# Block products for the last chunk's second layer, and transposes of the third chunk on TensorE

## The chip, the cores and the metric

One core of a Trainium2 chip. The metric is the time of one execution in device microseconds; the median of three runs of the kernel before is 212.14 us (211.63 to 212.49).

## What is computed

Attention with four sink keys and a window of 128, for 4 batches, 8 heads, 768 positions and head size 64, then a layer norm and a two-layer MLP with a residual:

```
scores = scale * q @ k^T;  keep where key < 4 or 0 <= row - key < 128
a = softmax(scores);  x = (a @ v), heads side by side      # 4 x 768 x 512
xn = (x - mean) / sqrt(var + 1e-6) * g_ln
out = x + relu(xn @ w_ch1) @ w_ch2                         # 512 -> 2048 -> 512
```

## The kernel before

The 3072 tokens are cut into 24 tiles of 128 and 12 chunks of two tiles; three chunks are one batch. For each chunk the kernel loads q and k (`nat`, L722, casting loads that POOL issues), transposes them so that the head size lies on the partitions (`kT`, `qT`), scores, exponentiates (ACT), masks and multiplies with v on TensorE, and normalises on VectorE: `x` (L1046), mean and variance (L900, L902), 1/sigma by a power on POOL (L910, L911), and `xc` (L907 without 1/sigma, L914 with it). `xc` is transposed into `xnt`. The MLP of the chunk has a first layer (`ph`, L1062: 64 matmuls of 128x256, `w1` against `xnt`), a relu into four `h1` tiles (L1073 on ACT, L1075 on VectorE), and a second layer.

From chunk 3 on, attention runs in blocks (`block`, L939): block t multiplies the probabilities of tile t-1 with v (L976 to L992) and then scores tile t (L1003, and L1011 for the sinks, in even tiles). Block 8 thus finishes tile 7, the last one that chunk 3's first layer needs, and scores the first tile of chunk 4.

The transposes of `xc` come in two kinds (`normalise`, L897). Chunks below `x_by_dma` (2 here) use four TensorE transposes a tile (L922); the eviction multiplies by `g_ln` (L933 on VectorE, L934 on ACT). The other chunks use a DMA transpose issued by SP (L925, issued through L595). These have no eviction, so `g_ln` must be in `w1`: after the last chunk with TensorE transposes, 16 operations scale `w1` in place (L1217 on VectorE, L1218 on ACT).

The second layer comes in two kinds. `second` (L1154) multiplies `h1` with `w2`, 16 matmuls for each tile or cut (L1167), then one fused operation adds the residual and multiplies by 1/sigma (L1175), and a store follows (L1179). The last tile is cut at column 320; the first cut is stored by ACT, the last by SP. `second_by_seven` (L1082) takes chunks 3 to 10. It regards the chunk's two tiles, the two halves of the 2048 hidden units and the two halves of the 512 output columns as 2x2 blocks, and makes the four output blocks from seven block products of eight 128x256 matmuls each (L1113) instead of eight. The sums that this needs are made once for `w2` (`w2t`, L1209), and in each chunk for `h1` (L1090, eight on VectorE). PSUM banks b0, b1, b2 hold the products; intermediate results are copied by ACT or VectorE (L1119) or added to an earlier copy (L1123), and `x` is added at the end (L1150). For these chunks `xc` has 1/sigma in it.

What sets the order: every operation is given to a planner (`Plan.run`, L114) with its possible engines, a cost and a priority (a due time). The planner lists the operations of each engine in the order of its own schedule, and the chip executes them so, with semaphores. TensorE, SP and the others each work through one list; a DMA transpose waits on SP behind whatever stands ahead of it. PSUM tiles (`one`, four banks; `pair`, two double banks) and SBUF tiles come from rings.

Of the kernel before, what the change touches and what calls it, by code (L numbers as in the profile page):

```python
# [10 lines left out]
ALU = mybir.AluOpType  # L11
# [194 lines left out]
def dve(n, per=1.04):  # L206
    t = 0.067 + 0.001 * per * n
    return (t, t + 0.09)


def fix(occ, extra=0.09):
# [8 lines left out]
HW_S = (0.75, 0.8, 1.2)  # L220
HW_X = (0.75, 0.2, 1.2)
# [9 lines left out]
NEVER = -1e9  # L231
BIG = 3.3e38

PAR = dict(gk=(5, 4), gv=(4, 5), strict=400.0, win=0.4, tr=-8.0, sc=-5.0, sc1=-2.0, av=2.0, blk=-8.0, step=10.0, trx=9.0, by_dma=4, x_by_dma=2,
           w1p=(1.6, 2.6, 2.7, 2.8), pm=3, w2p=(4.5, 4.51, 4.52, 4.53), apart=2, vs0=(2.0, 13.0), by_tile=0, vp=(0.0, 0.1, 2.0, 2.1, 4.55, 4.56), ld1=0.05, t0=0.8, warm=7.9, pm0=-40.0, w1g=17.0, gtt=1.25, seven=3, lead=(0, 0, 0, 2, 4, 9), w2t=-4.0, at7=(0.5, 1.5, 2.5, 3.5, 4.5, 6.5, 7.5))


# [134 lines left out]
def kernel(  # L372
# [12 lines left out]
    nc = tc.nc  # L385
# [4 lines left out]
    RB = S // 128  # L390
# [6 lines left out]
    NC = B * RC  # L397
# [7 lines left out]
    P = Plan()  # L405
# [110 lines left out]
    def negs(e):  # L516
# [18 lines left out]
         writes=[gr_b], dma=HW_T)  # L535
# [136 lines left out]
    def chunk(c):  # L672
# [37 lines left out]
        else:  # L710
            both = []
            for nm, src, bT in (("k", k, kT_b), ("q", q, qT_b)):
                T = Buf(f"{nm}T{c}", nm + "T")
                bT[c] = T
                if c < PAR["by_dma"]:
                    both.append((nm, src, T, ld + (0.1 if nm == "q" else 0.0)))
                    continue
                for i in range(2):
                    nat = Buf(f"{nm}n{c}{i}", "nat")
                    ap = src[b, :, 256 * R + 128 * i:256 * R + 128 * (i + 1), :].rearrange("h p d -> p h d")  # L720
                    P.op(f"{nm}ld{c}{i}", {"POOL": (0.87, 0.9)}, ld + 0.01 * i + (0.1 if nm == "q" else 0.0),
                         lambda e, nat=nat, ap=ap: G.dma_start(nat.t, ap), writes=[nat], dma=SW_N, after=gate(c))  # L722
                    P.op(f"tr{nm}{c}{i}", {"SP": (1.2, 1.2)}, d + 0.01 * i, lambda e, T=T, nat=nat, i=i: dma_t(
                        T.t[:, :, 128 * i:128 * i + 128], nat.t.rearrange("p h d -> p (h d)")),
                        reads=[nat], writes=[T], dma=HW_X, after=[trx_op[2 * c - 3]] if c > PAR["by_dma"] and nm == "q" else [])
            if both:
                by_pairs(c, both, d)
        if R == 0:
# [353 lines left out]
    def second_by_seven(c, T, h1):  # L1082
# [63 lines left out]
        for i, t in enumerate((t0, t1)):  # L1146
            b, r, x = t // RB, t % RB, x_b[t]
            done = Buf(f"of{t}")
            tail["sum", t] = P.op(f"o{t}", {"POOL": (1.1, 1.2), "DVE": dve(512, 1.06)}, T + 9 + i, lambda e, i=i, x=x: (
                V if e == "DVE" else G).tensor_tensor(ot[i].t, ot[i].t, x.t, op=ALU.add), reads=[ot[i], *oo[i], x], writes=[done])  # L1150
            P.op(f"st{t}", {"SP": (0.54, 0.59)}, T + 9.1 + i, lambda e, i=i, b=b, r=r: nc.sync.dma_start(
                out[b, 128 * r:128 * (r + 1), :], ot[i].t), reads=[ot[i], done], dma=HW_S)

    def second(c, T, h1):  # L1154
        for i in range(2):
# [90 lines left out]
    t = PAR["t0"]  # L1246
# [67 lines left out]
```

## Time and profile before

| | |
|---|---|
| runs | 212.49, 211.63, 212.14 us, median 212.14 |
| profiled execution | 211.49 us, of which the span is 210.0 |
| TensorE busy | 201.6 us |
| VectorE, ACT, POOL busy | 151.7, 121.4, 115.9 us |
| granted TensorE clock | 1.0 |

The span is the time from the first to the last instruction or transfer that the profile shows; the rest of the execution lies around it. Rows of a timeline give the start in us from the beginning of the span, the duration, the engine, the line, the operation, and in square brackets the idle time before it with what ended it. SPq, ACTq and POOLq are the issue of transfers, "DMA" in the chain of waits is a transfer from its issue to its landing. Rows of a group of instructions give the total busy time, the mean of one in ns, and the idle time before them.

### The profile page before, as it was taken

How to read it: one execution, taken by the hardware profiler on the slowest of the kernel's cores; microseconds unless marked ns; L12 is line 12 of the kernel's file. 1: busy time of each engine (PE TensorE's matmuls, PEld its weight loads, DVE VectorE, ACT ScalarE, POOL GpSimd, SP SyncE). 2: the span in 40 equal slices, each digit the busy share in tenths (PEclk: the TensorE clock that was granted, in tenths of full speed). 3: DMA queues.
4: the chain of work that ended last, by engine and by line, in shares of the span. 5: the costliest groups of instructions: out<-in, count | busy, mean ns of one | idle time of the engine just before them, and what ended most of it. 6: DMA issues, size and time to landing. Idle time of an engine off the chain costs nothing.

```text
span 210.0 us, 7046 instructions
## 1 busy us (share of the span) xinstructions
PE 201.6 (96%) x2891; PEld 161.7 (77%) x2891; DVE 151.7 (72%) x413; ACT 121.4 (58%) x212; POOL 115.9 (55%) x170
## 2 busy tenths in 40 slices
PE   7799999999989899899999999999999999999994
PEld 2458975755865688688888888888888888888853
DVE  5599867998845669888789688778778778773121
ACT  3798688283762475386475565665664764453610
POOL 7969942479979757846856792793732102410000
PEclk9999999999999999999999999999999999999999
DMA  5999999999999999999999999999994221120203
GB/s 146 195 186 199 190 208 200 169 187 142 163 193 125 153 153 130 124 204 149 76 185 152 77 158 184 85 152 171 94 174 101 78 78 25 59 71 3 100 0 108
DMA packets 105643, 28.05 MB, mean 134 GB/s; under 512 B 94852, under 2 KB 102664, under 8 KB 105608
## 3 DMA queue, kind: packets, MB, share of 16 engines
q0 software_dynamic: 70960, 13.18, 96.6%
q1 hardware_dynamic: 33448, 13.71, 37.6%
q10 hardware_dynamic: 1200, 0.69, 1.2%
q8 instruction: 23, 0.38, 0.8%
q14 instruction: 12, 0.10, 0.2%
HBM read 27.43 MB, written 6.29 MB: 161 GB/s over the span
## 4 chain that ended last, share of the span: by engine, by line
PE 81%; DMA 11%; DVE 4%; ACT 1%; issue 1%; POOL 1%; ACTq 0%; DVEq 0%; POOLq 0%
PE one L1062 37%; PE one L1113 22%; PE one L1167 11%; DMA xnt<-xc 5%; DMA qT<-nat 4%; DMA natf<-in_q_dram 3%; PE pair L1003 2%; PE one L976 2%; PE one L983 1%; PE one L992 1%; DVE st L900 1%; PE pair L1011 1%; DVE x L892 1%; PE pair L623 1%; PE pair L749 1%
## 5 line engine op out<-in xcount | busy, mean ns | idle before, releaser
L1062 PE MATMUL one<-xnt,w 128*128 128x256 bf16 x768 | 88.4, 273 | 1.6 <-DMA xnt<-xc 1.6
L1062 PEld LDWEIGHTS <-w 128*128 128x128 bf16 x768 | 74.2, 98 | 11.6 <-issue 2.3
L1073 ACT ACTIVATE h<-one 128x512 bf16<-128x512 f32 x92 | 54.8, 599 | 37.2 <-PE one L1062 36.0
L664 POOL DMA_DIRECT2D vn<-in_v_dram x59 | 39.2, 689 | 8.5 <-DMA w<-in_moe_w_ch_dram 6.9
L910 POOL TENSOR_SCALAR st<-st 128x1 f32<-128x1 f32 x24 | 9.8, 410 | 49.4 <-DVE st L902 48.9
L1021 ACT ACTIVATE pe<-pair 128x768 bf16<-128x768 f32 x36 | 27.3, 808 | 15.4 <-PE pair L1003 15.1
L1167 PE MATMUL one<-w,h 128*128 128x512 bf16 (+2 forms) x144 | 29.5, 356 | 0.0
L1167 PEld LDWEIGHTS <-h 128*128 128x128 bf16 x144 | 13.4, 98 | 12.0
L1113 PEld LDWEIGHTS <-h 128*128 128x128 bf16 x192 | 18.4, 98 | 2.7 <-issue 0.3
L1119 ACT COPY tx<-one 128x256 f32<-128x256 f32 x24 | 8.9, 372 | 18.4 <-PE one L1113 18.4
L911 POOL TENSOR_TENSOR st<-st,mhalf 128x1 f32<-128x1 f32 x24 | 16.3, 678 | 2.0
L900 DVE BATCH_NORM_STATS2 st<-x 128x6 f32<-128x512 bf16 x24 | 16.7, 694 | 0.8
L1113 PE MATMUL one<-w,h 128*128 128x256 bf16 x128 | 16.6, 273 | 0.1
L1113 PEld LDWEIGHTS <-sb 128*128 128x128 bf16 x156 | 14.8, 98 | 2.0
L1046 DVE TENSOR_TENSOR x<-one,rec 128x256 bf16<-128x256 f32 x36 | 15.3, 424 | 1.2
L722 POOL DMA_DIRECT2D nat<-in_k_dram x16 | 15.1, 950 | 1.3 <-DMA natp<-in_q_dram 1.3
L1150 DVE TENSOR_TENSOR ot<-ot,x 128x512 f32<-128x512 f32 x15 | 10.4, 692 | 7.2 <-ACT ot L1119 7.0
L722 POOL DMA_DIRECT2D nat<-in_q_dram x16 | 14.4, 912 | 0.0
L1175 DVE SCALAR_TENSOR_TENSOR ot<-one,st,x 128x512 f32<-128x512 f32 (+2 forms) x9 | 6.2, 691 | 11.2 <-PE one L1167 9.9
L1026 DVE TENSOR_TENSOR pe<-pe,band 128x768 bf16<-128x768 bf16 x24 | 12.0, 540 | 0.0
L914 DVE TENSOR_SCALAR xc<-x,st 128x512 bf16<-128x512 bf16 x16 | 6.6, 412 | 7.3 <-POOL st L911 7.3
L1123 DVE TENSOR_TENSOR ot<-one,tx 128x256 f32<-128x256 f32 x24 | 9.5, 418 | 2.6 <-PE one L1113 1.6
(145 smaller groups left out, 290.6 us busy)
## 6 DMA issues: line engine op xcount, KB each, us to landing
out_dram<-ot SPq DMA_DIRECT2D x23, 256.0 KB
w<-in_moe_w_ch_dram POOLq DMA_DIRECT2D x6, 512.0 KB, 12.3
nat<-in_k_dram POOLq DMA_DIRECT2D x16, 128.0 KB, 5.0
nat<-in_q_dram POOLq DMA_DIRECT2D x16, 128.0 KB, 5.7
vn<-in_v_dram POOLq DMA_DIRECT2D x44, 32.0 KB, 5.1
w<-in_moe_w_ch_dram POOLq DMA_DIRECT2D x4, 256.0 KB, 11.9
vn<-in_v_dram POOLq DMA_DIRECT2D x15, 64.0 KB, 5.2
natp<-in_k_dram POOLq DMA_DIRECT2D x3, 256.0 KB, 12.1
```

The costliest lines, as they stand in the source:

```text
L664: P.op(f"vld{t}_{i}", {"POOL": (0.8, 0.85)}, prio + 0.001 * i, lambda e, p0=p0, n=n, hs=hs, src=src: G.dma_start(m.t[p0:p0 + n, hs, 0:64], ...
L722: lambda e, nat=nat, ap=ap: G.dma_start(nat.t, ap), writes=[nat], dma=SW_N, after=gate(c))
L900: P.op(f"bn{t}", {"DVE": fix(0.60)}, d + 0.12, lambda e: V.bn_stats(st.t[:, 8:14], x.t), reads=[x], writes=[st, mv])
L911: G.tensor_tensor(st.t[:, 16:17], st.t[:, 17:18], mhalf, op=ALU.pow)),
L1021: nc.scalar.activation(pes[j].t.rearrange("p a b -> p (a b)")[:, 0:768].rearrange("p (a b) -> p a b", a=2), pps[j].t[:, :, 0:384], AF.Exp, ...
L1026: V.tensor_mul(at_s, at_s, band[j] if r > 1 else edge[r][j].unsqueeze(1).to_broadcast([128, 4, 192]))
L1046: P.op(f"x{t - 1}{u}", {"DVE": dve(256)}, d + 0.051 + 0.002 * u, lambda e, u=u, rc=rc, pv=pv: V.tensor_tensor(x.t[:, 256 * u:256 * u + 256 ...
L1062: nc.tensor.matmul(ph.t[:, 256 * s:256 * s + 256], lhsT=w1[ht // 4][:, j, 128 * (ht % 4):128 * (ht % 4 + 1)], rhs=xnt.t[:, j, :], start=j ...
L1073: nc.scalar.activation(dst, ph.t, AF.Relu)
L1113: nc.tensor.matmul(bank.t[:, 0:256], lhsT=left[p](m)[:, a, :], rhs=right[p](m)[:, a, :], start=new and m + a == 0, stop=m + a == 4, skip_g ...
L1150: V if e == "DVE" else G).tensor_tensor(ot[i].t, ot[i].t, x.t, op=ALU.add), reads=[ot[i], *oo[i], x], writes=[done])
L1167: nc.tensor.matmul(pc.t[:, 0:wd], lhsT=h1[s].t[:, 256 * ii + 128 * i:256 * ii + 128 * i + 128], rhs=w2[s][:, ii, sl], start=ht == 0, stop= ...
```

## The change

Two things.

The last chunk (11) goes by seven products too. It has an order of its own (`last_by_seven`): products 1, 7, 2, 6, 4, 5, 3, where 1, 6 and 5 add up in bank b0, 7, 2, 4 and 3 have a bank each, and every addition to `x` or to an earlier result is made by VectorE straight from the bank, so that no operation follows the last product but one addition of 256 columns and its store. Three stores take the place of the last chunk's three: half of tile 22 on SP, all of tile 23 on ACT, and the other half of tile 22 last, on SP.

`x_by_dma` goes from 2 to 3: chunk 2's two tiles are transposed on TensorE, and the 16 scalings of `w1` follow chunk 2's first layer instead of chunk 1's. The planner's lists change with it. On TensorE, block 8 now stands after 40 of the 64 matmuls of chunk 2's first layer (it stood behind all 64 and four matmuls of the second layer), block 10 after 32 of chunk 3's first layer (40 before), and blocks 12 and 14 each eight first-layer matmuls later. On SP the two transposes of chunk 2 are gone, and chunk 4's two query transposes stand together ahead of the store of tile 3, which stood between them. The other value, `opool=0`, keeps the choice of engines as it was.

```diff
-PAR = dict(gk=(5, 4), ..., by_dma=4, x_by_dma=2,
+PAR = dict(last7=1, opool=0, gk=(5, 4), ..., by_dma=4, x_by_dma=3,
...
     def by_seven(c):
-        return PAR["seven"] <= c < NC - 1
+        return PAR["seven"] <= c < NC - (0 if PAR["last7"] else 1)
...
         at = PAR["at7"]
+        if c == NC - 1:
+            return last_by_seven(t0, t1, ot, oo, (b0, b1, b2, Buf(f"b3_{c}", "one"), Buf(f"b4_{c}", "one")),
+                                 (k1, k6, k5, Buf(f"k12_{c}", "tx")), product, T)
...
+    def last_by_seven(t0, t1, ot, oo, b, k, product, T):
+        c, lo, hi, (b0, b1, b2, b3, b4), (k11, k21, k22, k12) = NC - 1, slice(0, 256), slice(256, 512), b, k
+        x0, x1 = x_b[t0], x_b[t1]
+
+        def plus(name, bank, dst, other, reads, writes):
+            return P.op(f"{name}_{c}", {"DVE": dve(256, 1.06)}, T, lambda e: V.tensor_tensor(
+                dst(), bank.t[:, 0:256], other(), op=ALU.add), reads=[bank, *reads], writes=writes)
...
+        product(1, b0, T + 0.1, True)
+        o1 = plus("k11", b0, lambda: k11.t, lambda: x0.t[:, lo], [x0], [k11])
+        product(7, b2, T + 0.2, True)
+        plus("k21", b2, lambda: k21.t, lambda: x1.t[:, lo], [x1], [k21])
+        plus("k22", b2, lambda: k22.t, lambda: x1.t[:, hi], [x1], [k22])
+        product(2, b1, T + 0.3, True)
+        plus("o11", b1, lambda: ot[0].t[:, lo], lambda: k11.t, [k11], [ot[0], oo[0][0]])
+        store(f"st{t0}0", "SP", t0, lo, [ot[0], oo[0][0]])
+        product(6, b0, T + 0.4, after=[o1])
+        o6 = plus("k21d", b0, lambda: k21.t, lambda: k21.t, [k21], [k21_done])
+        product(4, b3, T + 0.5, True)
+        tail["sum", t0] = plus("o21", b3, lambda: ot[1].t[:, lo], lambda: k21.t, [k21, k21_done], [ot[1], oo[1][0]])
+        product(5, b0, T + 0.6, after=[o6])
+        plus("o22", b0, lambda: ot[1].t[:, hi], lambda: k22.t, [k22], [ot[1], oo[1][1]])
+        store(f"st{t1}", "ACT", t1, slice(0, 512), [ot[1], oo[1][0], oo[1][1]])
+        plus("k12", b0, lambda: k12.t, lambda: x0.t[:, hi], [x0], [k12])
+        product(3, b4, T + 0.7, True)
+        plus("o12", b4, lambda: ot[0].t[:, hi], lambda: k12.t, [k12], [ot[0], oo[0][1]])
+        store(f"st{t0}1", "SP", t0, hi, [ot[0], oo[0][1]])
```

More of the change, by code (lines that the diff above doesn't have):

```diff
@@ L232 @@
 BIG = 3.3e38
-PAR = dict(gk=(5, 4), gv=(4, 5), strict=400.0, win=0.4, tr=-8.0, sc=-5.0, sc1=-2.0, av=2.0, blk=-8.0, step=10.0, trx=9.0, by_dma=4, x_by_dma=2,
+PAR = dict(last7=1, opool=0, gk=(5, 4), gv=(4, 5), strict=400.0, win=0.4, tr=-8.0, sc=-5.0, sc1=-2.0, av=2.0, blk=-8.0, step=10.0, trx=9.0, by_dma=4, x_by_dma=3,
            w1p=(1.6, 2.6, 2.7, 2.8), pm=3, w2p=(4.5, 4.51, 4.52, 4.53), apart=2, vs0=(2.0, 13.0), by_tile=0, vp=(0.0, 0.1, 2.0, 2.1, 4.55, 4.56), ld1=0.05, t0=0.8, warm=7.9, pm0=-40.0, w1g=17.0, gtt=1.25, seven=3, lead=(0, 0, 0, 2, 4, 9), w2t=-4.0, at7=(0.5, 1.5, 2.5, 3.5, 4.5, 6.5, 7.5))
@@ L724, in chunk @@
                         T.t[:, :, 128 * i:128 * i + 128], nat.t.rearrange("p h d -> p (h d)")),
-                        reads=[nat], writes=[T], dma=HW_X, after=[trx_op[2 * c - 3]] if c > PAR["by_dma"] and nm == "q" else [])
+                        reads=[nat], writes=[T], dma=HW_X, after=[trx_op[2 * c - 3]] if c > PAR["by_dma"] and nm == "q" and 2 * c - 3 in trx_op else [])
             if both:
@@ L1148, in second_by_seven @@
             done = Buf(f"of{t}")
-            tail["sum", t] = P.op(f"o{t}", {"POOL": (1.1, 1.2), "DVE": dve(512, 1.06)}, T + 9 + i, lambda e, i=i, x=x: (
+            tail["sum", t] = P.op(f"o{t}", {"POOL": (1.1, 1.2)} if PAR["opool"] else {"POOL": (1.1, 1.2), "DVE": dve(512, 1.06)}, T + 9 + i, lambda e, i=i, x=x: (
                 V if e == "DVE" else G).tensor_tensor(ot[i].t, ot[i].t, x.t, op=ALU.add), reads=[ot[i], *oo[i], x], writes=[done])
@@ L1152, in second_by_seven, with store @@
                 out[b, 128 * r:128 * (r + 1), :], ot[i].t), reads=[ot[i], done], dma=HW_S)
+    def last_by_seven(t0, t1, ot, oo, b, k, product, T):
[4 more added lines that the diff above has]
+                dst(), bank.t[:, 0:256], other(), op=ALU.add), reads=[bank, *reads], writes=writes)
+        def store(name, e, t, sl, reads):
+            bb, r = t // RB, t % RB
+            P.op(name, {e: (0.54, 0.59)}, T + 9, lambda e: (nc.sync if e == "SP" else nc.scalar).dma_start(
+                out[bb, 128 * r:128 * (r + 1), sl], ot[t - t0].t[:, sl]), reads=reads, dma=HW_S)
+        k21_done = Buf(f"k21d_{c}")
+        product(1, b0, T + 0.1, True)
[16 more added lines that the diff above has]
+        plus("o12", b4, lambda: ot[0].t[:, hi], lambda: k12.t, [k12], [ot[0], oo[0][1]])
+        tail["ot"], tail["oo"] = ot[0], oo[0][1]
+        store(f"st{t0}1", "SP", t0, hi, [ot[0], oo[0][1]])
     def second(c, T, h1):
```

## The prediction

> **What bounds the kernel now.** I read the shares of the engines first, then who TensorE waited for.
>
> ```profile
> span 210.0 us, 7046 instructions
> PE 201.6 (96%) x2891; PEld 161.7 (77%) x2891; DVE 151.7 (72%) x413; ACT 121.4 (58%) x212; POOL 115.9 (55%) x170
> PE one L1062 <- DMA xnt<-xc: 1.6, 2, 1.0
> PE pair L1011 <- DMA qT<-nat: 0.7, 1, 0.7
> ```
>
> TensorE is busy for 201.6 of 210.0 us. After the start it waits three times only, 2.3 us in all, each time for a DMA transpose. So the time moves by matmul work that goes or comes, by these waits, and by what follows the last matmul. The timeline of TensorE (start, duration, line, shape, count) has the stage of the waits:
>
> ```profile
> 52.34 7.16 PE L1062 MATMUL one<-xnt,w 128*128 128x256 bf16 x64
> 59.33 1.03 PE L1167 MATMUL one<-w,h 128*128 128x512 bf16 x4
> 60.20 0.41 PE L976 MATMUL one<-vn,pe 128*128 128x65 bf16 x8
> 61.97 0.29 PE L1011 MATMUL pair<-qT,kts 128*32 128x128 bf16 x8 [0.66 <-DMA qT<-nat]
> 62.20 4.49 PE L1167 MATMUL one<-w,h 128*128 128x512 bf16 x20
> 66.53 0.41 PE L976 MATMUL one<-vn,pe 128*128 128x65 bf16 x8
> 67.58 1.90 PE L1167 MATMUL one<-w,h 128*128 128x512 bf16 x8
> 70.11 4.53 PE L1062 MATMUL one<-xnt,w 128*128 128x256 bf16 x40 [0.63 <-DMA xnt<-xc]
> 74.48 0.41 PE L976 MATMUL one<-vn,pe 128*128 128x65 bf16 x8
> 85.21 1.03 PE L1062 MATMUL one<-xnt,w 128*128 128x256 bf16 x8 [0.98 <-DMA xnt<-xc]
> ```
>
> L976 opens a block: block 8 at 60.20, 9 at 66.53, 10 at 74.48; L1011 ends it where there are sinks. The waits stand in block 8 (queries of chunk 4), before chunk 3's first layer, and before chunk 4's. The rows also give prices by their starts: a 128x256 matmul of L1062 costs (59.33-52.34)/64 = 0.109 us, a 128x512 one (66.53-62.20)/20 = 0.2165, block 9 67.58-66.53 = 1.05. Block 8 reaches its L1011 at 61.97-0.66 = 61.31, 1.11 after its start. The chain of work names the transfers behind the waits, and the SP queue shows when they were issued:
>
> ```profile
> 54.52 7.41 DMA qT<-nat
> 65.03 4.95 DMA xnt<-xc
> 79.37 5.71 DMA xnt<-xc
> 43.24 3.39 SPq L595 DMA_TRANSPOSE xnt<-xc  x2
> 53.89 0.53 SPq L1179 DMA_DIRECT2D out_dram<-ot  x1
> 54.52 1.28 SPq L595 DMA_TRANSPOSE qT<-nat  x1
> 76.78 2.50 SPq L595 DMA_TRANSPOSE kT<-nat  x2
> 79.37 1.22 SPq L595 DMA_TRANSPOSE xnt<-xc  x1
> ```
>
> The end, in a timeline of all engines:
>
> ```profile
> 193.63 6.28 PE L1062 MATMUL one<-xnt,w 128*128 128x256 bf16 x56
> 199.75 7.11 PE L1167 MATMUL one<-w,h 128*128 128x512 bf16 x48
> 199.95 0.60 ACT L1073 ACTIVATE h<-one 128x512 bf16<-128x512 f32 x1 [0.28 <-PE one L1062]
> 206.33 0.38 ACTq L1179 DMA_DIRECT2D out_dram<-ot  x1
> 206.97 0.42 DVE L1175 SCALAR_TENSOR_TENSOR ot<-one,st,x 128x192 f32<-128x192 f32 x1 [0.67 <-PE one L1167]
> ```
>
> The last matmul ends by 206.97, the last sum at 207.39, and the store after it fills the 2.6 us to 210.0.
>
> **Part one: the last chunk.** The 48 matmuls of L1167 take 206.97-199.75 = 7.22 us. Seven products are 56 of 128x256, and a full row of them stands just above: 199.75-193.63 = 6.12. So 1.10 us less on TensorE, if nothing waits. What could wait is VectorE, which gets eight sums and nine additions where three fused operations stood (the third row is of SP, for the end of this part):
>
> ```profile
> L1090 DVE TENSOR_TENSOR sb<-h,h 128x512 bf16<-128x512 bf16 x10 | 4.2, 423 | 2.7 <-ACT h L1073 2.7
> L1123 DVE TENSOR_TENSOR ot<-one,tx 128x256 f32<-128x256 f32 x24 | 9.5, 418 | 2.6 <-PE one L1113 1.6 <-ACT tx L1119 1.1
> L595 SPq DMA_TRANSPOSE xnt<-xc x20: 1189/1202/1325, 43.2 to 182.4; - x20
> ```
>
> The last relu ends at 200.55, 0.80 after the products begin. From there VectorE has eight steps in a row (two sums, three additions to tokens, one output, one sum, the addition that frees the bank of products 1 and 6), 0.43 each with the gap: done 4.25 to 4.35 after the begin. Product 5 needs that bank at 5 x 0.875 = 4.37. I take a wait of 0.1; bounds 0 and 0.5 (one operation late). Products 2, 3, 4, 7 have banks of their own and never wait for an eviction. Last come one addition of 256 columns (0.42, as the 0.42 of the 192 columns now) and a store of 128 KB instead of 96 KB, with one of 256 KB (now 160 KB) less than 1 us ahead on ACT's queue. This I take at 0.2, between 0 and 0.5. Chunk 11's xc now waits for POOL's 1/sigma (about 1.2 us, as from 69.57 to 70.78 in the POOL rows below); the last of its transposes goes out at 182.4 and is wanted at 193.63, which hides it; were that cover gone it would cost the 1.2. Tail: -1.10 + 0.1 + 0.2 = **-0.8** (-1.1 to -0.1).
>
> **Part two: chunk 2 on TensorE.** Added: two groups of four transposes. Removed: the two DMA transposes issued at 43.24.
>
> ```profile
> 20.34 0.22 PE one L922 x4
> L922 PE MATMUL one<-ident,xc 128*128 128x128 bf16 x16 | 1.6, 220 | 0.4 <-DVE xc L907 0.4
> L933 DVE TENSOR_TENSOR xnt<-one,gt 128x512 bf16<-128x512 bf16 x3 | 2.0, 685 | 0.7 <-PE one L922 0.7
> L1217 DVE TENSOR_SCALAR w<-w,gt 128x512 bf16<-128x512 bf16 x10 | 2.9, 350 | 0.0
> L1218 ACT ACTIVATE w<-w,gt 128x512 bf16<-128x512 bf16 x6 | 4.2, 735 | 0.0
> ```
>
> In the chain of waits (first row) such a group of four holds TensorE for 0.22 us; two cost 0.45. Sixteen with a mean of 220 ns are busy for only 1.6 us in all, so they overlap, and the 220 is a latency. The Trainium skill ("TensorE: Matmul & The Clock Gate", Part 4: PE-mode transpose) puts one 128x128 transpose at about 275 ns inside a kernel; eight one after the other would be an estimated 2.2 us, 1.75 more than my term. The trace disagrees: four pass in 0.22.
>
> Their evictions (0.69 on VectorE, four small ones on ACT) end some 5 us before chunk 2's first layer. The sixteen scalings of w1 move from 31-47 us to behind chunk 2's first layer: 10 x 0.35 on VectorE and 6 x 0.7 on ACT between about 54 and 66 us, needed at the first matmul of chunk 3 near 69. Cost nothing; without that cover a few tenths.
>
> The order of TensorE changes with it, and this decides: block 8 now comes after 40 matmuls of chunk 2's first layer instead of 64. It starts at 52.34 + 0.45 + 40 x 0.109 = 57.16 and wants chunk 4's queries at 57.16 + 1.11 = **58.27**, not 61.31. When do they land? Call that X; now it is 54.52 + 7.41 = 61.93. Three things pull it forward: two transposes fewer ahead in the queue, the store of 53.89 moved behind, and less traffic for the loads that feed it:
>
> ```profile
> 46.79 1.85 POOL L722 DMA_DIRECT2D nat<-in_q_dram  x2
> DMA to landing us min/median/max: 4.7/4.7/4.7
> nat<-in_q_dram POOLq DMA_DIRECT2D x16, 128.0 KB, 5.7
> 69.57 0.43 POOL L910 TENSOR_SCALAR st<-st 128x1 f32<-128x1 f32 x1 [1.14 <-DVE st L902]
> 70.78 1.98 POOL L722 DMA_DIRECT2D nat<-in_k_dram  x2
> ```
>
> The second query load is issued near 47.7; with 4.7 to 5.7 us to land (the first load of this pair took 4.7, the median of all is 5.7) its transpose can go at 52.4 to 53.4, and it takes one of the three durations above, 4.95 to 7.41. X lies in 57.4 to 60.8; with 53.0 and the middle duration, 5.71, X = **58.7**: a wait of 0.4 in block 8.
>
> From X on: L1011 0.27, 24 matmuls of L1062 2.62, 24 of L1167 5.20, so block 9 starts at X + 8.09 = 66.8 (now 66.53). Then 1.05 + 8 x 0.2165: chunk 3's first layer at X + 10.9 = 69.6, half a microsecond earlier, and its own transpose, whose block came 2.6 us sooner, no longer stops it. Chunk 4's point came 85.21-0.98-70.11 = 14.1 us later, so TensorE could be there at X + 25.0 = 83.7. But that transpose hangs on block 9 through another chain: POOL's 1/sigma (69.57) releases the key loads (70.78), these the key transposes on SP (76.78, 2.50), and behind them in the same queue stands the one that is waited for (79.37). With that distance kept the wait ends at 85.21 + 0.26 = 85.5. Between 83.7 and 85.5 I take 84.7: contention eases a little, and xc is ready earlier. Middle: 84.7-85.21 = **-0.5** (-1.9 with TensorE alone deciding and X at or below 58.3, to +2.3 at X = 60.8). Later chunks show no waits now, and their order changes only by eight matmuls around a block.
>
> **The sum**: -0.5-0.8 = -1.3 us. Against the profiled execution, 211.49 (span 210.0 and 1.49 around it), that is 210.2. The median of the runs shown is 212.14, 0.65 above it; on it the forecast is **210.8**.
>
> **Rivals.**
> - *Slower: the queries come as late as now.* Block 8 arrives 3.0 us sooner and stops until 61.93; block 9 then starts at 70.0, 3.5 late, and chunk 4's transpose hangs on that. 3.5-0.8 = +2.7, 214.8. Against it: the queue is shorter by three entries. For it: 7.41 us in flight, the longest of the three. It turns slower by over 0.5% from X = 60.3.
> - *The gain is given back at 85 us.* All DMA chains keep their distance and chunk 4 waits until 85.2 or a little after; the tail alone counts: 211.3 on the median.
> - *All three waits go.* -2.27 + 0.45-1.10 = -2.9: 209.2. Against it: the key transposes ahead on SP.
> - *Transposes at full latency.* If a TensorE transpose cannot overlap its neighbour, eight of 0.22 cost 1.76 instead of 0.45: +1.3, the whole gain, 212.1. Against it: the 0.22 per four. The Trainium skill's section named above would give this; the chain of this trace speaks against it.
> - *Not what it says*: the tail's VectorE chain runs a step late twice and eats half of the 1.1: 211.4.
>
> **Chances.** Forecast 0.45, all waits gone 0.12, given back 0.2, late queries 0.13, full latency 0.03, tail eaten 0.07. A measurement of this kernel tells about 0.5%, 1.06 us, from no change. The forecast's own spread lies across that line, four fifths of it beyond: faster 0.48, same 0.39, slower 0.13. Range 209.2 to 213.2: from all waits gone to X of about 60.3; beyond are the latest queries.
>
> **What would show it.** Right: last-chunk matmuls in 6.1 to 6.4 us; last sum about 0.95 earlier before the end; two L922 groups of 0.22 near 45 us; no wait of chunk 3 for xnt; a wait of at most 1 us at L1011 near 58.3; chunk 4's first layer near 84.7. Wrong: queries landing after 60 us; gaps between products 6, 4, 5 for VectorE; a store that ends over 3 us after the last sum; new waits of chunk 5, whose blocks come eight matmuls later.

## The result and the profile after

The changed kernel takes 213.14 us (median; 213.01 to 213.85), the kernel before, run beside it, 211.91 (211.63 to 212.49). The ratio is 1.0065, with a 95% interval from 1.0038 to 1.0091: slower by 1.2 us, where 1.3 us less was forecast. The profiled execution took 213.85 us, with a span of 212.4.

First the head of the page:

```profile
span 212.4 us, 7099 instructions
...
PE 201.1 (95%) x2907; PEld 163.4 (77%) x2907; DVE 157.3 (74%) x427; ACT 122.6 (58%) x217; POOL 116.1 (55%) x170
```

And what TensorE waited for DMA (us in total, times, longest):

```profile
PE one L1062 <- DMA xnt<-xc: 0.9, 1, 0.9
PE pair L1003 <- DMA qT<-nat: 0.9, 1, 0.9
PE pair L1011 <- DMA qT<-nat: 0.4, 1, 0.4
```

TensorE has 0.5 us less work, and its waits for DMA are 2.2 us (2.3 before). Yet the span is 2.4 us longer. So I looked for where the distance to the kernel before opens. The middle, in TensorE's timeline:

```profile
57.17 0.41 PE L976 MATMUL one<-vn,pe 128*128 128x65 bf16 x8
...
58.80 0.54 PE L1003 MATMUL pair<-qT,kT 64*64 64x128 bf16 x32 [0.86 <-DMA qT<-nat]
59.73 0.29 PE L1011 MATMUL pair<-qT,kts 128*32 128x128 bf16 x8 [0.39 <-DMA qT<-nat]
...
67.77 0.41 PE L976 MATMUL one<-vn,pe 128*128 128x65 bf16 x8
...
70.56 3.66 PE L1062 MATMUL one<-xnt,w 128*128 128x256 bf16 x32
...
85.34 1.05 PE L1062 MATMUL one<-xnt,w 128*128 128x256 bf16 x8 [0.91 <-DMA xnt<-xc]
...
193.81 6.28 PE L1062 MATMUL one<-xnt,w 128*128 128x256 bf16 x56
```

Block 8 starts at 57.17, the queries are waited for until 59.73, chunk 3's first layer no longer waits, chunk 4's waits until 85.34 (85.21 before), and the last 56 of chunk 11's 64 first-layer matmuls start at 193.81 (193.63 before). In this execution nothing is won or lost up to there. The end, in a timeline of all engines:

```profile
199.92 1.04 PE L1113 MATMUL one<-w,h 128*128 128x256 bf16 x8
...
205.60 0.60 PE L1113 MATMUL one<-w,natc 128*128 128x256 bf16 x4
...
205.82 0.38 ACTq L1167 DMA_DIRECT2D out_dram<-ot  x1
206.23 0.43 DVE L1162 TENSOR_TENSOR ot<-one,tx 128x256 f32<-128x256 f32 x1
206.69 0.33 SPq L1167 DMA_DIRECT2D out_dram<-ot  x1
...
206.81 0.19 PE L1274 MATMUL one<-ones_f,ot 128*1 128x1 f32 x2 [0.61 <-DVE ot L1162]
```

The last sum ends at 206.66, 0.73 us earlier than before (207.39), though the last chunk began 0.18 later: seven products save the 0.9 us. But the span goes on for 5.7 us behind it, where it went on for 2.6. The whole loss stands in these 3.1 us, in which no engine computes. The granted TensorE clock doesn't explain it: it is 1.0 up to 210.0 us, and falls only in the idle 2.3 us behind that (mean 0.53). The timeline doesn't list branches; the instructions of one source line do. The line is the test at the program's end, L1274 before and L1312 after. First the kernel before:

```profile
L1274 POOLq COMPARE_BRANCH  x1: 59/59/59, 205.2 to 205.2; - x1
...
L1274 PEldq COMPARE_BRANCH  x1: 388/388/388, 208.0 to 208.0; - x1
```

Then the changed kernel:

```profile
L1312 POOLq COMPARE_BRANCH  x1: 59/59/59, 205.9 to 205.9; - x1
...
L1312 PEldq COMPARE_BRANCH  x1: 3697/3697/3697, 207.5 to 207.5; - x1
```

What SP waited for at the program's last line, a row of the changed kernel's waits:

```profile
SPq L1347 <- PEq L1312: 2.4, 1, 2.4
```

And its transfers from 208.5 to 208.6 us by queue (packets, MB, share of the engines):

```profile
q8 instruction: 1, 0.02, 80.0%
```

TensorE's branch (PEldq is the sequencer of its weight loads, min/median/max in ns) took 388 ns before and 3697 ns now, from 207.54 to 211.24, and SP, which closes the program, waited 2.4 us for it.

What that branch is must be told, since neither the change nor the prediction touches it. The kernel is written for the usual case. VectorE counts the rows for which that case doesn't hold (L1260 to L1262; the lines of this paragraph are those of the changed kernel), POOL moves the counts to one partition, VectorE sums them into a flag (`gflag`, L1270 and L1271), and every engine loads the flag and branches: usually over the code of a general fallback (`general`), of which the code of some 750 matmul calls (counted in the kernel's text) lies between TensorE's branch and its target. Code is fetched by DMA in blocks; queue q8 is by its count TensorE's (23 packets of 16 KB in the page before, one for about every 250 of its instructions, and one behind its branch), q14 that of the others (8 KB each). A hint at the start of the program (`mark_branch_hint_location`, L1302) announces the branch. In the changed kernel no block for TensorE is fetched between 192 us and the branch. One is fetched at 208.54, 1.0 us after the branch has begun, and 2.7 us later TensorE goes on. The Trainium skill ("Runtime: NRT & Kernel Launch", section "Instruction fetch mechanics") says that a taken branch whose target is not among the loaded code blocks must wait for a fetch. The trace agrees: the branch takes 3.3 us more than in the kernel before. That the late block is the target's is inferred from its time; the trace doesn't name addresses.

Behind the wait at the branch a second, smaller delay is hidden. In the table below, "landing" is the last completion of the last store, counted from the end of the last sum: 1.65 us before, 2.22 now.

### The profile page after: what moved, and what is told of

Its sections match the earlier page's. It is cut to its first block, busy times and chain, and to the rows that moved or that the text cites. A ratio compares the mean times of both kernels' runs of the same rounds, so it can differ in the third digit from the quotient of the medians.

```text
span 212.4 us, 7099 instructions
## 1 busy us (share of the span) xinstructions
PE 201.1 (95%) x2907; PEld 163.4 (77%) x2907; DVE 157.3 (74%) x427; ACT 122.6 (58%) x217; POOL 116.1 (55%) x170
## 4 chain that ended last, share of the span: by engine, by line
PE 82%; DMA 8%; DVE 4%; ACT 1%; issue 1%; POOL 1%; ACTq 0%; POOLq 0%
PE one L1062 36%; PE one L1113 24%; PE one L1205 10%; DMA qT<-nat 3%; DMA natf<-in_q_dram 3%; DMA xnt<-xc 2%; PE pair L1003 2%; PE one L976 2%; PE one L983 1%; PE one L992 1%; DVE st L900 1%; PE pair L1011 1%; PE one L922 1%; DVE x L892 1%; PE pair L623 1%
## 5 line engine op out<-in xcount | busy, mean ns | idle before, releaser
L1113 PEld LDWEIGHTS <-h 128*128 128x128 bf16 x216 | 20.7, 98 | 2.8
L1205 PE MATMUL one<-w,h 128*128 128x512 bf16 x96 | 22.4, 380 | 0.0
L1113 PE MATMUL one<-w,h 128*128 128x256 bf16 x144 | 18.7, 273 | 0.0
L1113 PEld LDWEIGHTS <-sb 128*128 128x128 bf16 x176 | 16.7, 98 | 2.3
L911 POOL TENSOR_TENSOR st<-st,mhalf 128x1 f32<-128x1 f32 x24 | 16.9, 704 | 2.0
L1205 PEld LDWEIGHTS <-h 128*128 128x128 bf16 x96 | 9.0, 98 | 9.6 <-DMA w<-in_moe_w_ch_dram 0.3
L914 DVE TENSOR_SCALAR xc<-x,st 128x512 bf16<-128x512 bf16 x18 | 7.6, 422 | 8.3 <-POOL st L911 8.2
L1113 PE MATMUL one<-natf,sb 128*128 128x256 bf16 x88 | 12.6, 273 | 0.0
L1113 PEld LDWEIGHTS <-natc 128*128 128x128 bf16 x112 | 10.9, 98 | 1.3
```

What stands on the lines that cost most here:

```text
L911: G.tensor_tensor(st.t[:, 16:17], st.t[:, 17:18], mhalf, op=ALU.pow)),
L1113: nc.tensor.matmul(bank.t[:, 0:256], lhsT=left[p](m)[:, a, :], rhs=right[p](m)[:, a, :], start=new and m + a == 0, stop=m + a == 4, skip_g ...
L1205: nc.tensor.matmul(pc.t[:, 0:wd], lhsT=h1[s].t[:, 256 * ii + 128 * i:256 * ii + 128 * i + 128], rhs=w2[s][:, ii, sl], start=ht == 0, stop= ...
```

## The experiments

Two theories at first: **A (code)**, TensorE's last branch waits for its target's code, and **B (stores)**, 256 KB on ACT's queue right ahead of SP's last 128 KB make the end late. All results in one table. "Fetch" is the start of the last TensorE block that was fetched ahead of the end of the branch, relative to the branch's start; "none" means that none came between 193 us and the end of the branch. The time of the kernel before is the one measured beside.

| kernel | us | before | ratio (95%) | branch us | fetch | landing | end after the last sum |
|---|---|---|---|---|---|---|---|
| before | | | | 0.39 | none | 1.65 | 2.61 |
| changed | 213.14 | 211.91 | 1.0038 to 1.0091 | 3.70 | +1.0 | 2.22 | 5.70 |
| a_again | 212.66 | 211.46 | 1.0016 to 1.0083 | 3.37 | +1.0 | 2.23 | 5.37 |
| a_last | 211.33 | 211.48 | 0.9977 to 1.0013 | 0.40 | none | 2.31 | 3.50 |
| a_mid | 211.02 | 211.46 | 0.9977 to 1.0029 | 0.39 | none | 1.65 | 2.73 |
| b_nohint | 214.10 | 211.65 | 1.0101 to 1.0210 | 3.41 | +1.0 | 1.65 | 5.23 |
| a_skip222 | 212.73 | 211.48 | 1.0015 to 1.0068 | 0.50 | -2.5 | 2.21 | 3.50 |
| b_skip34 | 211.35 | 211.48 | 0.9988 to 1.0033 | 0.39 | none | 1.66 | 2.62 |
| b_run34 | 211.68 | 211.48 | 0.9994 to 1.0028 | 1.41 | -1.0 | 2.17 | 3.17 |
| b_start34 | 211.23 | 211.48 | 0.9989 to 1.0042 | 0.50 | -3.6 | 1.65 | 2.63 |
| a_less18 | 212.54 | 211.46 | 1.0008 to 1.0071 | 0.39 | none | 2.28 | 3.49 |
| a_more34 | 211.37 | 211.46 | 0.9982 to 1.0020 | 0.50 | -2.4 | 2.25 | 3.49 |
| a_more8 | 212.97 | 211.40 | 0.9998 to 1.0077 | 3.60 | +1.0 | 2.26 | 5.62 |
| a_split | 210.66 | 211.48 | 0.9953 to 1.0002 | 0.50 | -2.3 | 2.24 | 3.53 |
| a_flag | 210.08 | 211.48 | 0.9915 to 0.9966 | 0.50 | -2.3 | 1.76 | 2.86 |
| a_both | 210.27 | 211.48 | 0.9920 to 0.9983 | 0.50 | -1.9 | 2.28 | 3.32 |
| a_late | 213.87 | 211.40 | 1.0070 to 1.0157 | 0.50 | -2.6 | 5.12 | 6.22 |
| a_last_flag | 210.84 | 211.40 | 0.9949 to 1.0001 | 0.40 | none | 1.74 | 2.72 |
| a_flag_bare | 212.60 | 211.65 | 0.9996 to 1.0089 | 3.54 | +1.2 | 1.74 | 5.56 |
| a_flag2 | 210.35 | 211.65 | 0.9915 to 0.9978 | 0.50 | -2.3 | 1.75 | 2.84 |

### The parts alone, and the change once more

```diff
-           ..., by_dma=4, x_by_dma=3,      # a_last
+           ..., by_dma=4, x_by_dma=2,
-PAR = dict(last7=1, opool=0,               # a_mid
+PAR = dict(last7=0, opool=0,
```

> The last chunk's part alone: chunk 2 is transposed by DMA as before, the last chunk runs as seven block products. The jump and its target lie 17 instructions further than before, half of the change's 34. B (stores): the last sum about 0.9 earlier, the end still 5.7 after it: +2.2, 214.1, with nothing at the jump. A (code): the jump is either 0.4 us (then the end is 0.3 to 0.4 earlier than before, the stores landing 2.2 after the last sum instead of 1.6: 211.5) or 3.7 (214.1 again, but then TensorE's jump shows it).

> Chunk 2's transposes on TensorE alone; the last chunk as before (three cuts). The jump lies 17 instructions further than before. Block 8 at 57.2, TensorE waits for chunk 4's queries to about 59.7 and at 85 us for chunk 4's transpose; chunk 11's first layer at 193.8 against 193.6. A2: jump 0.4, time 0.0 to 0.4 above the kernel before. B (late stores): the stores are those of the kernel before, so the same 0.0 to 0.4. If the transposes cost their full latency (the rival of the prediction): +1.3.

> The changed kernel once more, unchanged, beside the other three on one chip and in more executions: A2: the jump of TensorE between 1.5 and 4 us in the profiled execution, times spread over 1.5 us or more, 0.8 to 1.6 above the kernel before. B: the same mean with a spread of 0.4. D: some executions at the level of the kernel before or under it.

Each part alone is within 0.3% of the kernel before; together they cost 1.2 us again. The loss is in neither part. With each part alone the branch takes 0.40 and 0.39 us, with both 3.37. Half of theory B falls too: `a_last` has the changed kernel's stores and not its long end. But it keeps 0.9 of the 3.1 us (3.50 against 2.61), the late landing among them, and so the 0.9 us of the earlier sum buys nothing. For `a_again`, the ten executions differ by more than 2 us, from 210.59 up; a branch that is caught out in most executions and not in all would do this.

### Where the code lies

```diff
     with tc.If(bad > 0, label="fits"):                        # a_skip222: 111, b_skip34: 17
+        for _ in range(111):
+            nc.tensor.matmul(pairs[0][0:1, 0, 0:1], lhsT=junk[:, 0:1], rhs=junk[:, 0:1], start=True, stop=True)
...
             elif o is not order_last:                         # b_run34, a_more34: 17, a_more8: 4
+                if o.name == "hold":
+                    for _ in range(17):
+                        nc.tensor.matmul(pairs[0][0:1, 0, 0:1], lhsT=junk[:, 0:1], rhs=junk[:, 0:1], start=True, stop=True)
                 o.emit(o.eng)
...
-                for n in o[0]:                                # a_less18
+                for n in [n for n in o[0] if n > 256]:
...
-                for n in o[0]:                                # b_start34
+                for n in o[0] + [1] * (5 if len(o[0]) == 6 else 2):
```

> The changed kernel with 222 more TensorE instructions (111 matmuls of one column) at the head of the fallback code that the last branch jumps over; they are never executed, and nothing that is executed changes. Theory A (code): the 3.1 us lost after the last sum are TensorE's last jump, 3.70 us after the change and 0.39 before, because its target has to be loaded first, and the 34 TensorE instructions that the change adds moved it within the blocks of 256 instructions (16 KB) in which code is fetched. If it is the target's place that decides (A1), 34 + 222 = 256 puts the target back where it was in its block: jump 0.4 us, end set by the last store (landed at 208.9, the end about 1.0 later), span 212.4 - 2.4 = 210.0, time about 210.7. If the jump's own place decides (A2): jump 3.7, time 213.1. Theory B (stores): 256 KB on ACT's queue and 128 KB on SP's less than 1 us apart make the end late: unchanged, 213.1.

> The kernel before with 34 more TensorE instructions (17 matmuls of one column) in the fallback code that is jumped over, never executed. A1 (the target's place decides): the jump takes 3.7 us instead of 0.39, from 208.04 to 211.7, the end about 1.1 later: span 212.8 instead of 210.0, time about 214.6. A2 (the jump's own place decides) and B (stores): 211.9, unchanged.

> The kernel before with 17 matmuls of one column (34 TensorE instructions) executed in the half microsecond in which TensorE waits for the last sum. The jump and its target lie as in the changed kernel, everything else is the kernel before. A (code, either place): jump 3.7 us, time 214.6, up to 0.4 more for the added matmuls. B (stores): 211.9 to 212.3, the jump 0.4.

`b_skip34`: moving the target alone does nothing. `a_skip222` gave two sets of times: 210.75 twice, once in the profiled execution, where a block was fetched 2.5 us ahead of the branch, 212.0 to 213.5 in seven others, and 215.16 in one. It executes what the changed kernel does, and its one profiled branch took 0.50 us. So the target's place doesn't decide, and the times say that the same program has both outcomes. In `b_run34` the added instructions do bring one more block, 1.0 us ahead of the branch, and the branch takes 1.41 us. It is over at 209.16, before the last store lands (209.28), so the stores cover it; but that landing is itself 0.5 us later than before, to which I come back.

> The changed kernel with 18 TensorE instructions fewer: of the warm-up matmuls in the idle time at the start, whose results nobody reads, the nine of 256 columns are left out. Jump and target come 18 instructions earlier, within one place of where they lie in the kernel with the last chunk's part alone, whose jump took 0.4 us with no code fetched between 191 us and the jump. Theory A2 (the jump's own place): a boundary of a fetched block lies in the last 17 instructions ahead of the changed kernel's jump; with 18 fewer it is not reached, the target's block is fetched at about 190 us, the jump takes 0.4 and the time is 0.6 to 1.0 below the kernel before (as the two runs in which the kernel with 222 unexecuted instructions took 210.75), and within 0.4 us of itself from run to run; if the clock at the start suffers from the missing warm-up, up to 0.5 is lost there. Theory B (stores): 1.2 above the kernel before, as the change. Theory D (chance: the fetch of the target's block is slow in some executions whatever the place): a mix of both, some executions 2 us above the others.

> The changed kernel with 34 TensorE instructions more (17 matmuls of one column) executed while TensorE waits for the last sum, where they took 0.56 us in the kernel before. The jump moves 34 instructions on, so the boundary lies 34 to 51 instructions ahead of it instead of under 17, in the last product. A2: the fetch of the target's block starts about 1 us earlier, at 206 or before; the jump takes 0.4 to 1.5 us, the time is 0.6 to 1.0 below the kernel before, or a few tenths worse. B: 1.2 above the kernel before. D: mixed times.

> The kernel before with 34 TensorE instructions more (17 matmuls of one column) spread over the warm-up of the first 11 us, where TensorE idles; nothing else changes, and the code ahead of the jump is that of the kernel before. Theory A2 (the jump's own place): the boundary lies under 17 instructions ahead of the jump, as in the changed kernel; a code block is fetched within 3 us of the jump, which takes 1.5 to 3.7 us instead of 0.39, and the time is 0.5 to 2 above the kernel before, with a wider spread. If the jump is slow only together with the changed kernel's stores (theory B): within 0.2 of the kernel before.

> The changed kernel with 8 TensorE instructions more (4 matmuls of one column, 0.13 us) executed while TensorE waits for the last sum. Open is why the same place of the jump gave a late fetch in the changed kernel (207.6 and 208.5 in two profiles) and an early one in the kernel before with 34 instructions at its start (204.0). Theory W (the wait): in the changed kernel the boundary lies behind TensorE's wait for the last sum, within 6 instructions of the jump, and the fetch starts only after that wait; 8 more instructions behind the boundary and ahead of the wait put it ahead of the wait: fetch near 204, jump 0.5 us, 211.4 as with 34. Theory N (no such wait, the boundary lies in the last product): the fetch comes 0.1 to 0.4 us earlier at most, the jump takes 2 to 3.5 us in most executions, 212.2 to 212.8 and a spread of over 1.5.

For `a_more34`, the branch's rows:

```profile
L1315 POOLq COMPARE_BRANCH  x1: 59/59/59, 205.1 to 205.1; - x1
...
L1315 PEldq COMPARE_BRANCH  x1: 497/497/497, 206.8 to 206.8; - x1
```

And its transfers from 191 to 206.7 us, with the one fetched block:

```profile
q8 instruction: 1, 0.02, 0.4%
```

With 34 instructions more the block comes ahead of the branch, and the 1.2 us are gone: 211.37, level with the kernel before. With 18 fewer the branch is short as well, and no block is fetched late. (The time of `a_less18` tells nothing: chunk 11's first layer starts at 195.1, over 2 us late, with a mean granted clock of 0.984, because the warm-up matmuls are missing at the start.) With 8 more it is long, so theory W is wrong: the 8 instructions should have brought the boundary ahead of the wait. And `b_start34`, with the branch where the changed kernel has it, has a short one. So A2 in its simple form, the branch's place alone, is wrong too.

What the place does decide shows in the number of TensorE's blocks. The pages of all kernels with the branch 34 or more instructions further than before count 24 packets on q8, those with 0 to 17 more count 23 (all but `b_nohint`, below, with 24). So with 34 more, one more block falls due near the end. When it is requested, the place doesn't say: the table has it from 3.6 us ahead of the branch to 1.2 us behind its start.

```diff
-    for e in ("PE", "Activation", "Pool"):                    # b_nohint
+    for e in ("Activation", "Pool"):
         tc.mark_branch_hint_location("fits", hint="LikelyTaken", engines=[getattr(mybir.EngineType, e)])
```

> The kernel before without TensorE's prefetch hint for the last jump (one instruction at the start of the program; the hints of ScalarE and GpSimd stay). If the changed kernel's slow jump is one whose target's block was not loaded ahead, this gives the kernel before the same: no block fetched between 191 us and the jump, one 1.0 us after it begins, jump 3.3 to 3.7 us from 208.0, the end at 212.5 instead of 210.0: 213.4 to 213.9, in every execution. If the slow jump has another cause (the changed kernel's stores, or TensorE's queue): 211.4, jump 0.4.

The branch in `b_nohint`:

```profile
L1274 PEldq COMPARE_BRANCH  x1: 3413/3413/3413, 207.6 to 207.6; - x1
```

And the block that it waited for, in the transfers from 208.5 to 208.6 us:

```profile
q8 instruction: 1, 0.02, 64.2%
```

Without TensorE's hint, the kernel before shows the changed kernel's picture: no block ahead, one 1.0 us after the branch's start, 3.41 us, 2.45 us slower. So the slow branch is most likely one whose target was not loaded ahead in spite of the hint: leaving out the hint alone gives the same rows. What keeps the hint from working in most executions of the changed kernel, with 8 instructions more as well but not with 34 more or 17 or 18 fewer, stays open.

### The stores, and the flag

```diff
+        store(f"st{t1}0", "ACT", t1, lo, [ot[1], oo[1][0]])               # a_split: tile 23 in two,
         product(5, b0, T + 0.6, after=[o6])                               # on top of a_more34
...
-        store(f"st{t1}", "ACT", t1, slice(0, 512), [ot[1], oo[1][0], oo[1][1]])
+        store(f"st{t1}1", "ACT", t1, hi, [ot[1], oo[1][1]])
...
-        plus("o11", b1, ...)                                              # a_flag: the flag one sum
+        tail["sum", t0] = plus("o11", b1, ...)                            # earlier, on top of a_more34
-        tail["sum", t0] = plus("o21", b3, ...)                            # a_late: behind o22 instead
+        plus("o21", b3, ...)                                              # a_both: a_split and a_flag
```

> The changed kernel with the 34 executed instructions that keep the jump short (0.50 us, 211.37 against 211.46 before), and tile 23's store cut in two of 128 KB on ACT's queue: the first as soon as product 4's sum is there, some 0.9 earlier, so that 128 KB instead of 256 KB are less than 1 us ahead of the last store. If the 256 KB cost the last store its 0.6 (2.25 from the last sum to the landing, 1.65 before): landing about 1.75 to 1.9 after the last sum. If GpSimd's closing work (1.87 us, ended at 208.55, behind SP's 208.41) holds the end as well, only 0.1 of it is seen in the time; if not, 0.4 to 0.5. If the size of the last store itself (128 KB against 96 KB) is the cause: landing 2.2, no gain.

> The changed kernel with the 34 executed instructions, and the flag for the fallback summed one VectorE operation earlier, in an idle 0.45 us ahead of product 4's sum. GpSimd reads the flag and then needs about 4.1 us to the end of its closing work; that comes about 0.7 earlier and no longer holds the end, which is now set by the last store alone: 0.2 less than 211.37, if the closing theory is right; nothing if the landing sets the end anyway.

> Both: the store in two and the flag earlier. If the stores cost 0.4 to 0.5 and GpSimd's closing work 0.2, the two together give 0.6 to 0.7: about 210.7 to 210.8, 0.7 below the kernel before, the last landing 1.75 to 1.9 and the end 2.6 to 2.8 after the last sum (3.49 with neither). If neither theory holds: 211.4.

The operation `gflag` waits for `tail["sum", NT - 2]`, by which the kernel before meant tile 22's fused sum. `last_by_seven` sets it to product 4's sum. The flag's last operation ended 2.83 us ahead of the last sum's end before (204.56 to 207.39) and 1.39 ahead in the changed kernel; GpSimd's branch stands at 205.2 and 205.9. Moved back by one addition, into an idle 0.45 us of VectorE, it gives 210.08 us, 0.6% below the kernel before. The 256 KB on ACT are still there, so theory B is wrong. What was in the last store's way is seen in the traffic of the 1.8 us from the issue of the last store, in 40 slices of 45 ns (GB/s), with the packets by queue (q1 has SP's store). First `a_more34`, from 205.9:

```profile
GB/s 273 182 410 319 501 273 455 319 364 364 364 410 364 501 228 273 182 0 0 137 273 319 523 341 341 319 319 228 137 46 23 23 23 23 0 205 205 23 0 0
...
q1 hardware_dynamic: 144, 0.13, 21.4%
q14 instruction: 3, 0.02, 3.8%
```

Then `a_flag`, from 205.42:

```profile
GB/s 273 182 455 319 455 319 364 455 319 546 273 501 228 546 228 228 137 0 0 159 250 319 387 387 341 364 341 205 114 46 0 0 0 0 182 0 182 0 0 0
...
q1 hardware_dynamic: 144, 0.13, 21.3%
q14 instruction: 2, 0.02, 2.9%
```

And the branch in `a_flag`:

```profile
L1315 POOLq COMPARE_BRANCH  x1: 59/59/59, 203.7 to 203.7; - x1
...
L1315 PEldq COMPARE_BRANCH  x1: 502/502/502, 206.3 to 206.3; - x1
```

ACT's store fills the first 17 slices in both, SP's the next 12. In `a_more34` the store has a tail of single packets, 23 GB/s each: four slices by themselves, two beside a code block's 182, and one more. And one code block more (q14) lies in the stretch: at 206.91, 1.0 us after the issue, in the middle of the store. It takes 0.31 us, and the last packet of the store ends 0.35 us later than in `a_flag`. Of the store's 16 completions, 15 come by 1.75 us after the last sum and one at 2.25. In `a_flag` that block is at 204.86, ahead of both stores, and the tail is gone: all 16 come by 1.76. I put the block down to GpSimd, whose branch alone lies so early (1.1 to 1.8 us ahead of it); the trace doesn't name the engine.

`b_run34` shows the same without the changed kernel's stores. It has those of the kernel before (160 KB on ACT, 96 KB on SP), and the block is TensorE's, of 16 KB, 0.4 us ahead of the issue of the last store at 207.14. Its traffic from 206.5 us in slices of 60 ns:

```profile
GB/s 0 0 0 0 273 0 0 149 235 363 384 363 363 341 235 107 22 0 0 21 0 0 21 0 98 205 329 320 303 218 137 34 21 26 26 26 26 137 137 0
...
q8 instruction: 1, 0.02, 2.4%
```

The block is the 273 in the fifth slice. A few packets of ACT's store straggle behind it (21 each), then some of SP's (26), and the landing is 2.17; the kernel before has no stragglers there, and 1.65.

The rest of the rows' gain, 0.1 us (from the landing to the end 1.24 and 1.10, 0.96 before), is at the very end. GpSimd's long drain takes 1.87 us, and it ended at 208.55 in `a_more34`, behind SP's own at 208.41. With the early flag it is done 0.2 us ahead of SP's (207.21 against 207.43). So the rows give 0.63 of the 1.3 us between `a_more34` and `a_flag`; in the two profiles the 56 matmuls of chunk 11 also start 0.48 apart, which the flag cannot have done. Cutting ACT's store in two brings nothing to the landing (2.24 and 2.28). In `a_both`, in spite of the early flag, GpSimd's block comes at 205.08 among the packets of the first half, which is sent earlier there: 14 of that half's completions come by 0.03 us after the last sum, the last at 1.03. How this reaches SP's store is not shown. The median of `a_split` is lower than that of `a_more34` by 0.7, but the intervals of their ratios overlap, and its end has no row that would explain a gain.

> The changed kernel with the 34 executed instructions (211.37) and the flag summed later instead of earlier: on VectorE behind the last sum, about 2.0 us later than there. Theory F (GpSimd's code is fetched about 1.8 us after the flag, 8 KB on one of the DMA engines, and the last store's pieces on that engine wait for it): the fetch now comes after the store, which lands 1.65 to 1.8 after the last sum instead of 2.25. GpSimd's closing work ends 4.1 us after the flag, at about 210.5, and holds the end: 1.6 to 2.0 slower, about 213.2. If instead the 256 KB ahead cost the store its 0.6: landing 2.25 still. If GpSimd's closing work doesn't hold the end: 211.4 or less.

> The last chunk's part alone (chunk 2 by DMA), with the flag summed one VectorE operation earlier; the jump lies where it took 0.40 us. The accounting says: last sum 0.9 earlier as with the part alone (which measured 211.33 against 211.48 before), and with GpSimd's code fetch and closing work out of the way another 0.6 to 0.8: 210.6 to 210.8, 0.7 to 0.9 below the kernel before, landing 1.65 to 1.8 and the end 2.6 to 2.9 after the last sum. If the flag was worth its 1.3 only together with chunk 2's transposes or the padding: 211.3.

`a_late` is slower by 1.1%, but its landing refutes what was expected. Its end:

```profile
205.90 0.42 DVE L1162 TENSOR_TENSOR ot<-one,tx 128x256 f32<-128x256 f32 x1
...
206.54 0.14 DVE L1271 CAST flag<-n_sum 1x1 int32<-1x1 f32 x1
207.61 0.34 SPq L1167 DMA_DIRECT2D out_dram<-ot  x1
```

And the code blocks in the 3.6 us from the issue of its last store:

```profile
q14 instruction: 4, 0.03, 3.6%
q8 instruction: 1, 0.02, 3.0%
```

SP reads the flag ahead of the last store, so the store is issued 1.29 us after the last sum. Then five code blocks fall into its way, and it takes 3.83 us to land instead of 1.73: the same collision, larger. `a_last_flag` comes out by its rows as the accounting says: landing 1.74, end 2.72 after the last sum. The time, 210.84 us, is 0.56 below the kernel before, with an interval that just reaches 1.

> The changed kernel with the flag summed one VectorE operation earlier, without the 34 executed instructions. If jump and flag are two causes that add up, the landing is right (1.76 after the last sum) but the jump in most executions still takes 3.3 to 3.7 us from about 206.3, and holds the end: 212.0 to 212.8, spread over 2 us, with one or two executions of ten near 210.1. If the early flag also cures the jump: 210.1 in all.

> The best version once more beside the other two: the changed kernel with the flag one operation earlier and the 34 executed instructions: jump 0.50, landing 1.76 after the last sum, 210.0 to 210.4 against 211.4 for the kernel before.

Both causes have to go. With the early flag alone the landing is right, but the branch is still long and hides the gain (212.60, the changed kernel 212.66); with the short branch alone the time is 211.37; with both, 210.35 against 211.65, again 0.5% faster than the kernel before. `a_flag`, run twice, is below both the kernel before and the changed one.

## Why the prediction was wrong, point by point

**TensorE in the tail: nearly right.** In the chain of waits of the changed kernel the seven products stand as one piece:

```profile
200.08 6.13 PE one L1113 x56
```

There is no wait for VectorE among them. From the start of the first product (199.92) to that of the last sum (206.23) it is 6.31 us, against 7.22 for the 48 matmuls: 0.91 less, where 1.10 were expected without a wait and 1.0 with the wait of 0.1. The 1.10 set two measures side by side: the 7.22 runs to the sum, while the 6.12 for 56 narrow matmuls runs only from their start to the next matmul's start. To the end of the last sum it is 6.74 against 7.64: -0.90.

**The last stores: the term was mis-sized.** The step was "This I take at 0.2, between 0 and 0.5". It measures 0.57 in the landing (2.22 against 1.65), up to 0.66 in `a_last`, and with the close 0.89 (3.50 against 2.61). Its reason was wrong as well: not 256 KB ahead on another queue, but a code block among the store's packets and GpSimd's late close. Both follow from a step that `last_by_seven` moves and that the sum left out, the flag's. So the tail's -0.8 is -0.90 + 0.89, nothing, as `a_last` shows (0.9977 to 1.0013).

**TensorE's last branch: not in the sum.** +3.3 us of branch, of which 2.2 come out at the end (5.70 against 3.49 in `a_more34`). In the time it is 1.3 and 2.25: 212.66 in `a_again` against 211.37 in `a_more34`, 212.60 against 210.35 between `a_flag_bare` and `a_flag2`. No rival had it. The nearest sign named was "a store that ends over 3 us after the last sum"; the span does, the store doesn't. The rows of the line L1274 stood in the trace of before, with 388 ns, and the prediction doesn't read them.

**The middle: right on average, with steps mis-sized.** The queries were waited for until 59.73, where X was taken at 58.7 (bounds 57.4 to 60.8): the transfer took 6.49 us from 53.20 instead of 5.71 from 53.0. From there on the prediction's distances hold: block 9 at 67.77 (59.73 + 8.09 = 67.82), chunk 3's first layer at 70.56 (70.63). The two transfers in the chain of waits, then the transposes in TensorE's timeline:

```profile
53.20 6.49 DMA qT<-nat
...
80.01 5.29 DMA xnt<-xc
```

```profile
44.78 0.40 PE L922 MATMUL one<-ident,xc 128*128 128x128 bf16 x4
45.88 0.39 PE L922 MATMUL one<-ident,xc 128*128 128x128 bf16 x4
```

The two groups of transposes take 0.40 and 0.39 us. The prediction's 0.22 was a misreading: it is the part of a group that lies on the chain of waits, and the row beside it, 1.6 us for sixteen, gave 0.40 for four. So the term was 0.8 and not 0.45, and "full latency" (1.76 in all) is out all the same. The 275 ns a transpose of the Trainium skill ("TensorE: Matmul & The Clock Gate", Part 4) would make 2.2 us of the eight; the trace disagrees, with 0.8. In this one execution chunk 4 is at 85.34, as the rival "given back at 85 us" says. But over twelve profiles with chunk 2's transposes on TensorE (`a_less18` left out), chunk 4's first layer starts at 84.43 on average, over seven without at 84.98; the 56 matmuls of chunk 11 at 192.97 and 193.48. The middle is worth about -0.5, with a standard error of 0.2; single executions differ by over 1 us. That this is the forecast's figure to the tenth is partly luck, as two of its terms, X and the transposes, had been taken too small for the profiled execution.

**The sum.** -0.5 - 0.9 + 0.9, and 1.3 to 2.2 for the branch, give +0.8 to +1.7; measured +1.2. With the two ends mended, -0.5 - 0.9 + 0.25 = -1.15 by the rows, measured -1.4 and -1.3: what the forecast of -1.3 was, but for a kernel whose end stays out of the way.

## What to carry to other kernels

When a change shortens the end of a kernel, read everything that stands behind the last operation, branches and code fetches too; an end that was hidden behind the last store comes out when the store comes sooner. A change that adds instructions moves all code behind it, and a jump over a big block at the end can then wait for its code: 34 instructions added by themselves gave 0.5 and 1.4 us, and the changed kernel, with as many, 3.4 and 3.7. Look at it in the profile after every edit, and at the spread of the times. And find what hangs by name on an operation that is replaced (here the flag on `tail["sum", ...]`).

## What the runs showed of the hardware

- TensorE's taken branch over the fallback took 0.39 to 0.50 us where no block came late, and 3.4 to 3.7 where a block of 16 KB came 1.0 to 1.2 us after its start; a block fetched 1.0 us ahead of it left 1.41.
- The same executed instructions had either: 0.50 us in `a_skip222`, 3.70 and 3.37 in the changed kernel. The times of `a_skip222` (210.75 twice, 212.0 and more in eight) suggest that one program can have either, from one execution to the next; its branch was profiled once.
- One code block of 8 KB in the middle of a store of 128 KB delayed its landing by 0.5 us (2.25 against 1.76), one of 16 KB ahead of a store of 96 KB by as much (2.17 against 1.65); five blocks delayed one by 2.1 (3.83 against 1.73 from its issue).
- A second store on ACT's queue, 0.9 us behind another of 128 KB, took 0.65 and 1.03 us to issue instead of 0.38 (`a_split`, `a_both`).
